# Splitting the attention result straight from PSUM, and weight conversions without a rank

## The chip, the cores and the metric

The kernel runs on one core of a Trainium2 chip. The metric is the device time of one execution in microseconds (us); lower is better. A core has five engines with queues of their own: TensorE (PE), which multiplies matrices into PSUM, VectorE (DVE), ScalarE (ACT) and GpSimd (POOL) for work on tiles, and SyncE (SP), which here issues all transfers.

## The reference

The reference is a linear attention with decay, followed by two pairs of dense layers, all in float32; the weights of the layers are given in double precision.

```python
for t in range(S):                                  # B, H, S, D = 4, 8, 768, 48
    cur = einsum('bhd,bhe->bhde', u * k_t, v_t)
    y[:, :, t] = einsum('bhd,bhde->bhe', r_t, state + cur)
    state = w_t[..., None] * state + einsum('bhd,bhe->bhde', k_t, v_t)
x = y as [B * S, H * D]                             # 3072 tokens of 384
h = x @ w_in;  x = where(h >= 1, h, where(h <= -1, 0, (h + 1) ** 2 / 4)) @ w_out    # d_ff = 2048
h = x @ w2_in; return (h * sigmoid(1.702 * h)) @ w2_out
```

## The kernel before, in words

**Products in two parts.** For speed, PE multiplies a rounded format. To keep float32 accuracy, each operand is split into a high part, rounded to that format, and a low part, the difference: `xh` and `xl` for the tokens, `whi` and `wlo` for the weights, `gh` and `gl` for the hidden layer. Each product is then three: high by high, high by low, low by high.

**Steps.** Tokens come in 8 tiles of 384. A step `s` handles one tile and one of the 16 slices of 128 hidden units: `gemm1` (9 matmuls into the PSUM tile `hp`), the activation (for layer 0: DVE L701, ACT L702, DVE L714, which gives `t`; then ACT L695 `gh` and, a step later, POOL or DVE in turn L689 `gl`), and `gemm2` (9 matmuls) for step `s - 3`. Steps 0 to 127 are layer 0, 128 to 255 layer 1.

**Attention windows.** The attention is computed in 24 windows of 128 tokens, three to a tile. `window(n)` (L416) is a generator, cut by `yield` into about 13 slots: the scans of the decay on DVE (L433, L435), products on DVE and POOL, the transposes `tp` and the scores `sc` on PE (L479, L484), the masked copy on DVE (L489), then `kv` (L508) and `yt` (L514) on PE. `yt` is a PSUM tile of 128 x 4 x 128: for each half of the partitions (a head of a pair) 48 rows, padded to 64, and four pairs of heads. The layer wants three blocks of 128 rows, so the fourth pair's 48 rows go, 16 at a time, into the padding of the first three. This is done with six transfers (L536) inside the SBUF tile `xr`, a copy of `yt` by ACT (L533). After them, ACT rounds the first three blocks to `xh` (L547), and `xl` is the difference (L550), on DVE for the first six windows (`XL_N`) and on POOL for the others, one slot later.

**Gate.** `attn_slot` (L560) moves every window in flight by one slot. A window that has yielded `"x"` (L542) is held as long as its tile lies more than one ahead of the tile that the steps work on. Windows start 4 slots apart at first and then 8 apart; the steps of a tile call 24 slots. Windows of layer 0 up to the third are run ahead of step 0.

**Weights.** `load_w` (L140) brings a piece of 128 x 384 doubles from HBM into one of four buffers `wst`; there are 32 pieces for layer 0, two for each slice. `to_f32` and `wide` make float32 of it: DVE L653, ACT L654, DVE L655, POOL L657. `load_w` for the piece four further on follows when a piece has been read. `split_w` makes `whi` (ACT L168) and `wlo` (PE and ACT for the first ten pieces, then DVE and POOL in turn, L177). Ten pieces are converted ahead of step 0; step `f` of tile 0 calls for the pieces up to `2 * f + 2 + 6` (L278), so the last pair is called for at step 12.

**What sets the order.** Up to and with step 15 (tile 0) the instructions are put in order by a scheduler: it simulates the engines and gives each one, among what is ready, the instruction of the highest rank. The rank is the place in the program; `high_priority(x)` lifts it by `x` places. Windows 0 to 2 are lifted by 400 (`WP0`), the first ten pieces by 300 (`CP0`), and pieces 10 to 31 by 3000 (`CP1`, L277). From step 16 on (`manual_schedule`) the order is that of the program. The order of each engine's queue, SP's among them, is fixed when the kernel is built, and each queue works in order.

Lines that the change and the steps of the prediction touch: the `"x"` gate (L542, L566), the copy `xr` (L533), the transfers (L536), `xh` (L547), `xl` (L550), `split_x2` (L247), which gives layer 1 its two parts in tiles of the same tags, and `CP1` (L66, used in L277).

Of the kernel before, what the change touches and what calls it, by code (L numbers as in the profile page):

```python
# [9 lines left out]
F32 = mybir.dt.float32  # L10
F32R = mybir.dt.float32r
I32 = mybir.dt.int32
U32 = mybir.dt.uint32
AF = mybir.ActivationFunctionType
ALU = mybir.AluOpType
# [4 lines left out]
B, H, S, D = 4, 8, 768, 48  # L20
NT, DM, DFF = B * S, H * D, 2048
C = 64
W = 128
NP = H // 2
# [5 lines left out]
KD = DM // 128  # L30
# [8 lines left out]
TN = 384  # L39
# [22 lines left out]
XL_N = 6  # L62
F0 = 0
WP0 = 400
CP0 = 300
CP1 = 3000  # L66
MAXW = 6
GAP1 = 8
CHECK_LATE = True
# [13 lines left out]
@with_exitstack  # L83
def rwkv_mlp_mlp_kernel(ctx, tc, rkw_t, nat, v_l, w1, w2, r, k, v, w, u, mi, mo, m2i, m2o, out, force=False):
    nc = tc.nc
    dram = ctx.enter_context(tc.tile_pool(name="dram", bufs=1, space=DRAM))
    keep = ctx.enter_context(tc.tile_pool(name="keep", bufs=1))
    x2_d = dram.tile([128, KD, NT], F32, name="x2_d")
    w2_d = dram.tile([128, 2 * KF, DM], F32, name="w2_d")
    flag_i = keep.tile([1, 1], I32, name="flag_i")  # L90

    with ExitStack() as st:
        fast_path(st, tc, rkw_t, nat, v_l, w1, w2, u, out, x2_d, w2_d, flag_i, force)

    rv = nc.values_load(flag_i[0:1, 0:1], min_val=0, max_val=1)
    with tc.If(rv == 0):
        general_path(tc, r, k, v, w, u, mi, mo, m2i, m2o, out)


def fast_path(st, tc, rkw_t, nat, v_l, w1, w2, u, out, x2_d, w2_d, flag_i, force):  # L100
    nc = tc.nc
    one = st.enter_context(tc.tile_pool(name="one", bufs=1))
    p2 = st.enter_context(tc.tile_pool(name="p2", bufs=2))
# [118 lines left out]
            nc.scalar.activation(out=whi[f][q], in_=wf, func=AF.Copy)  # L222
            late.append((i, wf))

    xh, xl = {}, {}
    x2_t = {}
    accs = {}
    gq = {}
# [17 lines left out]

    def split_x2(i):  # L247
        x2 = x2_t.pop(i)
        h_ = p2.tile([128, KD, TN], F32R, tag="xh", name="x2h")
        l_ = p2.tile([128, KD, TN], F32R, tag="xl", name="x2l")  # L250
        nc.vector.tensor_copy(h_, x2)
        nc.vector.tensor_tensor(out=l_, in0=x2, in1=h_.bitcast(F32), op=ALU.subtract)
        xh[1, i], xl[1, i] = h_, l_
# [15 lines left out]
    def step(s):  # L269
        if s < NS:  # L270
# [5 lines left out]
            if l == 0 and i == 0:  # L276
                with hooks["prio"](CP1):  # L277
                    while nconv[0] < min(NPC, 2 * f + 2 + AHEAD):  # L278
# [38 lines left out]
        if s < NS:  # L317
# [15 lines left out]
            if last and f == 8:  # L333
                split_x2(0)
# [9 lines left out]
            if l == 1 and i + 1 < len(TILES2):  # L344
                if f == 4:
                    load_x2(i + 1)
                if f == 12:
                    split_x2(i + 1)

    with ExitStack() as sa:  # L350
        at = sa.enter_context(tc.tile_pool(name="at", bufs=1))
        a2 = sa.enter_context(tc.tile_pool(name="a2", bufs=2))
# [49 lines left out]
        def load_v(n):  # L402
            i = n % 2
            tv = a2.tile([128, NP, 2, D], F32, tag="vn", name="vn")
            nc.sync.dma_start(out=tv, in_=nat[n, :, 2 * MC * D:].rearrange("p (m h d) -> p m h d", h=2, d=D))
            vn_t[n] = tv
            for hh in range(2):
                p = slice(64 * (1 - hh), 64 * (1 - hh) + 64)
                nc.sync.dma_start(out=lt[i][p, hh], in_=v_l[n, hh])
# [6 lines left out]
        def window(n):  # L416
            i = n % 2
            b, j = divmod(n, WPB)
            ti, off = tile_of[n]
# [26 lines left out]
            def lt_s(hh, c):  # L446
                p = slice(64 * hh, 64 * hh + D)
                return lt[i][p, hh].rearrange("p (m c) e -> p m c e", c=NC2)[:, :, c, 0:D]

            def put(us):  # L450
                for hh in range(2):
                    p = slice(64 * hh, 64 * hh + D)
                    nc.gpsimd.tensor_tensor(out=lt_s(hh, 0), in0=us[p], in1=pcs[p, :, None].to_broadcast([D, NP, D]), op=ALU.mult)
# [43 lines left out]
            yield from idle(GAPS[1])  # L497
            if PUT == 2 and not first:
                put(carry.pop())
            kvt = ps_s.tile([128, NC2, NP, D], F32, tag="s", name="kv")  # L500
            kv = [kvt[:, c] for c in range(1 if last else NC2)]

# [7 lines left out]
            def mm_y(c):  # L510
                for m in range(NP):
                    for hh in range(2):
                        mc = m * NC2 + c
                        nc.tensor.matmul(out=yt[64 * hh:64 * hh + 64, m, c * C:(c + 1) * C], lhsT=lt[i][:, hh, mc, :], rhs=ra[hh][:, mc, :], start=True, stop=True)  # L514
# [9 lines left out]
            yt = ps_s.tile([128, NP, W], F32, tag="s", name="yt")  # L524
# [4 lines left out]
                carry.append(upd(1))  # L529
            yield from idle(GAPS[2])  # L530
            mm_y(1)
            xr = a2.tile([128, NP, W], F32, tag="xr", name="xr", bufs=1)
            nc.scalar.activation(out=xr, in_=yt, func=AF.Copy)  # L533
            for hh in range(2):
                for q in range(3):
                    nc.sync.dma_start(out=xr[64 * hh + D:64 * hh + 64, q, :], in_=xr[64 * hh + 16 * q:64 * hh + 16 * q + 16, 3, :])  # L536
            yield
            sq = vn.rearrange("p m h d -> p (m h d)")
            nc.scalar.activation(out=sq, in_=sq, func=AF.Square, accum_out=stat[:, n, 2:3])
            if n + 2 < NW:  # L540
                load_v(n + 2)
            yield "x"  # L542
            if off == 0:
                xh[0, ti] = p2.tile([128, KD, TN], F32R, tag="xh", name="xh")
                xl[0, ti] = p2.tile([128, KD, TN], F32R, tag="xl", name="xl")
            o = xh[0, ti][:, :, off:off + W]
            nc.scalar.activation(out=o, in_=xr[:, 0:KD, :], func=AF.Copy)  # L547
            if n >= XL_N:
                yield
            (nc.vector if n < XL_N else nc.gpsimd).tensor_tensor(out=xl[0, ti][:, :, off:off + W], in0=xr[:, 0:KD, :], in1=o.bitcast(F32), op=ALU.subtract)  # L550
            yield

        def idle(n):
# [6 lines left out]
        def attn_slot():  # L560
            n = started[0]
            if n < (NW if cur[0] >= 0 else MAXW) and n in vn_t and n in nat_t and (not queue or queue[-1][1] >= GAP[0]):
                started[0] += 1
                queue.append([window(n), 0, n, None])
            for e in list(queue):
                if e[3] == "x" and tile_of[e[2]][0] > cur[0] + 1:  # L566
                    continue
                try:
                    e[3] = next(e[0])
                    e[1] += 1  # L570
                except StopIteration:
                    queue.remove(e)
# [306 lines left out]
```

## Time and profile before

| what | us |
|---|---|
| median of 3 runs (lowest, highest) | 1003.78 (1003.73, 1005.83) |
| the profiled execution, its own time | 1002.71 |
| its span, from the first instruction to the last | 1001.0 |
| PE busy in the span | 945.8 |
| DVE, ACT, POOL busy | 562.0, 538.2, 393.4 |

The rows that the prediction rests on stand in a section below, in numbered groups. Times in them are from the start of the span. A row of a timeline has the start, the length, the engine, the line, what is written from what, and in brackets the idle time ahead of it with what ended it. In the rows by line, the first numbers behind the bar are the busy time of the group and the mean of one instruction in ns. Busy times of matmuls overlap, so a group's mean is longer than the distance between two starts.

### The profile page before, as it was taken

Reading aid. Unit: us, or ns where it says so; the run is one execution under the profiler, and the core shown is the slowest. Engines: PE = TensorE matmul, PEld = TensorE weight load, DVE = VectorE, ACT = ScalarE, POOL = GpSimd, SP = SyncE. Lnnn points to the kernel's source line nnn. Section 1 sums busy time; section 2 is a strip of 40 time slices with the busy share of each in tenths; the row PEclk is TensorE's granted clock in tenths of the full one; section 3 lists DMA queues with packets and bytes.
Section 4 is the critical chain, followed back from the end, with each engine's and each line's share of the span. In section 5 each row is a group of like instructions: output and inputs, shape, how many; then the busy total and the mean of one; then the engine's idle time right before and its main releaser. Section 6 shows DMA issues by size and latency. Waiting matters only on the chain.

```text
span 1001.0 us, 18691 instructions
## 1 busy us (share of the span) xinstructions
PE 945.8 (94%) x6976; PEld 906.6 (91%) x6976; DVE 562.0 (56%) x983; ACT 538.2 (54%) x1279; POOL 393.4 (39%) x416
## 2 busy tenths in 40 slices
PE   4656999999999999999999999999999999999997
PEld 2445889999999999999999999999999999999997
DVE  6899976776877767777745753323232323232321
ACT  4666545666666667665654565555455433333332
POOL 6788744555555456455432541111111111111111
PEclk8857999999999999999999999999999999999999
DMA  9886515445555445553203443322222101000000
GB/s 236 208 226 176 140 24 164 132 118 140 156 134 147 117 113 154 144 146 104 66 20 115 129 133 99 96 78 85 87 81 85 59 2 45 3 28 22 25 1 28
DMA packets 52228, 101.73 MB, mean 102 GB/s; under 512 B 8608, under 2 KB 31392, under 8 KB 52128
## 3 DMA queue, kind: packets, MB, share of 16 engines
q1 hardware_dynamic: 52128, 100.45, 35.8%
q8 instruction: 57, 0.93, 0.4%
q14 instruction: 43, 0.35, 0.1%
HBM read 83.51 MB, written 15.73 MB: 99 GB/s over the span
## 4 chain that ended last, share of the span: by engine, by line
PE 63%; DVE 13%; ACT 10%; DMA 5%; issue 5%; SPq 3%; POOL 0%; ACTq 0%; DVEq 0%
PE hp L664 29%; PE acc L682 20%; PE acc L673 10%; SPq L536 3%; DVE pi L433 2%; DMA rk<-rkw_t 2%; DMA xr<-xr 2%; ACT gh L695 2%; DVE t L714 2%; ACT ra L472 2%; DVE ra L489 2%; ACT t L702 2%; DVE pi L435 1%; PE kv L508 1%; PE yt L514 1%
## 5 line engine op out<-in xcount | busy, mean ns | idle before, releaser
L689 POOL TENSOR_TENSOR gl<-t,gh 128x384 fp32r<-128x384 f32 x128 | 132.5, 1035 | 497.0 <-ACT gh L695 465.5
L695 ACT ACTIVATE gh<-t 128x384 fp32r<-128x384 f32 x256 | 134.1, 524 | 171.6 <-DVE t L714 93.4
L725 DVE TENSOR_TENSOR t<-t,hp 128x384 f32<-128x384 f32 x128 | 70.9, 554 | 218.6 <-ACT t L720 218.1
L720 ACT ACTIVATE t<-hp 128x384 f32<-128x384 f32 x128 | 62.8, 491 | 145.8 <-PE hp L664 145.8
L673 PE MATMUL acc<-gl,whi 128*128 128x384 f32 x384 | 131.2, 342 | 2.5 <-DVE gl L689 2.5
L673 PE MATMUL acc<-gh,whi 128*128 128x384 f32 x384 | 131.7, 351 | 0.8 <-ACT ev L263 0.3
L673 PE MATMUL acc<-gh,wlo 128*128 128x384 f32 x384 | 130.2, 339 | 0.0
L682 PE MATMUL acc<-wlo,gh 128*128 128x384 f32 x384 | 129.7, 338 | 0.0
L682 PE MATMUL acc<-whi,gh 128*128 128x384 f32 x384 | 129.5, 337 | 0.0
L682 PE MATMUL acc<-whi,gl 128*128 128x384 f32 x384 | 129.3, 337 | 0.0
L689 DVE TENSOR_TENSOR gl<-t,gh 128x384 fp32r<-128x384 f32 x128 | 75.4, 589 | 63.5 <-ACT gh L695 62.8
L702 ACT ACTIVATE t<-t 128x384 f32<-128x384 f32 x128 | 66.4, 519 | 65.7 <-DVE t L701 65.4
L714 DVE TENSOR_TENSOR t<-t,hp 128x384 f32<-128x384 f32 x128 | 70.2, 548 | 54.0 <-ACT t L702 52.5
L664 PE MATMUL hp<-xh,whi 128*128 128x384 f32 x384 | 91.9, 348 | 3.2 <-DVE t L714 3.2
L664 PE MATMUL hp<-xl,whi 128*128 128x384 f32 x384 | 89.3, 341 | 5.0 <-DVE xl L550 5.0
L701 DVE TENSOR_SCALAR t<-hp 128x384 f32<-128x384 f32 x128 | 70.4, 550 | 39.9 <-PE hp L664 39.6
L664 PE MATMUL hp<-x2h,whi 128*128 128x384 f32 x384 | 88.8, 339 | 0.0
L664 PE MATMUL hp<-xh,wlo 128*128 128x384 f32 x384 | 88.7, 339 | 0.0
L664 PE MATMUL hp<-x2l,whi 128*128 128x384 f32 x384 | 88.5, 339 | 0.0
L664 PE MATMUL hp<-x2h,wlo 128*128 128x384 f32 x384 | 88.1, 337 | 0.0
L673 PEld LDWEIGHTS acc<-gh,whi 128*128 128x128 f32 x384 | 72.2, 189 | 5.0 <-ACT ev L263 2.3
L673 PEld LDWEIGHTS acc<-gl,whi 128*128 128x128 f32 x384 | 72.6, 189 | 3.0 <-DVE gl L689 2.6
(108 smaller groups left out, 1849.1 us busy)
## 6 DMA issues: line engine op xcount, KB each, us to landing
wst<-w SPq DMA_DIRECT2D x96, 384.0 KB, 3.3
rk<-rkw_t SPq DMA_DIRECT2D x48, 288.9 KB, 5.0
rkn<-nat SPq DMA_DIRECT2D x24, 384.0 KB, 4.8
lt<-v_l SPq DMA_DIRECT2D x48, 128.0 KB, 3.7
w_d<-wt SPq DMA_DIRECT2D x32, 192.0 KB, 4.3
w2f<-w_d SPq DMA_DIRECT2D x32, 192.0 KB, 2.5
vn<-nat SPq DMA_DIRECT2D x24, 192.0 KB, 3.4
x_d<-ev SPq DMA_DIRECT2D x24, 192.0 KB, 2.2
```

The lines of the kernel that those rows point to most:

```text
L433: nc.vector.tensor_tensor_scan(out=rr[:, WW:0:-1], data0=ws[:, WW:0:-1], data1=one_s[:, WW:0:-1], initial=0.0, op0=ALU.mult, op1=ALU.max)
L536: nc.sync.dma_start(out=xr[64 * hh + D:64 * hh + 64, q, :], in_=xr[64 * hh + 16 * q:64 * hh + 16 * q + 16, 3, :])
L664: nc.tensor.matmul(out=hp[:, 0:n], lhsT=win(a, f, kk), rhs=b[:, kk, 0:n], start=(i == 0), stop=(i == 3 * KD - 1))
L673: nc.tensor.matmul(out=acc[j][:, 0:n], lhsT=wout(a, f, j * 128, 128), rhs=b[:, 0:n], start=(f == 0 and i == 0), stop=(f == KF - 1 and i == 2))
L682: nc.tensor.matmul(out=o[:, 0:DM], lhsT=a[:, j * 128:(j + 1) * 128], rhs=wout(b, f, 0, DM), start=(f == 0 and i == 0), stop=(f == KF - 1 a ...
L689: eng.tensor_tensor(out=gl[:, 0:n], in0=t[:, 0:n], in1=gh[:, 0:n].bitcast(F32), op=ALU.subtract)
L695: nc.scalar.activation(out=gh[:, 0:n], in_=t[:, 0:n], func=AF.Copy)
L701: nc.vector.tensor_scalar(t[:, 0:n], hp[:, 0:n], scalar1=-1.0, scalar2=1.0, op0=ALU.max, op1=ALU.min)
L702: nc.scalar.activation(out=t[:, 0:n], in_=t[:, 0:n], func=AF.Square, bias=0.5, scale=0.5)
L714: nc.vector.tensor_tensor(out=t[:, 0:n], in0=t[:, 0:n], in1=hp[:, 0:n], op=ALU.max)
L720: nc.scalar.activation(out=t[:, 0:n], in_=hp[:, 0:n], func=AF.Sigmoid, scale=1.702)
L725: nc.vector.tensor_tensor(out=t[:, 0:n], in0=t[:, 0:n], in1=hp[:, 0:n], op=ALU.mult)
```

## The change

After the change, `yt` is not copied to `xr`. One SBUF tile `xx` holds both parts, each with the four blocks of a token tile. ACT writes the high part of `yt` straight from PSUM into it, DVE subtracts that from `yt` in PSUM into the low part, for all windows, and the six transfers of a window move 16 rows of both parts at once. `split_x2` uses tiles of the same tag. The gate `"x"` moves ahead of the `kv` product. `CP1` is 0, so the conversion of pieces 10 to 31 is no longer lifted.

```diff
@@ -63,7 +63,7 @@
 F0 = 0
 WP0 = 400
 CP0 = 300
-CP1 = 3000
+CP1 = 0
 MAXW = 6
 GAP1 = 8
 CHECK_LATE = True
@@ -222,7 +222,7 @@
             nc.scalar.activation(out=whi[f][q], in_=wf, func=AF.Copy)
             late.append((i, wf))
 
-    xh, xl = {}, {}
+    xh, xl, xx = {}, {}, {}
     x2_t = {}
     accs = {}
     gq = {}
@@ -246,8 +246,8 @@
 
     def split_x2(i):
         x2 = x2_t.pop(i)
-        h_ = p2.tile([128, KD, TN], F32R, tag="xh", name="x2h")
-        l_ = p2.tile([128, KD, TN], F32R, tag="xl", name="x2l")
+        x = p2.tile([128, 2, NP, TN], F32R, tag="xx", name="xx2")
+        h_, l_ = x[:, 0, 0:KD], x[:, 1, 0:KD]
         nc.vector.tensor_copy(h_, x2)
         nc.vector.tensor_tensor(out=l_, in0=x2, in1=h_.bitcast(F32), op=ALU.subtract)
         xh[1, i], xl[1, i] = h_, l_
@@ -497,6 +497,7 @@
             yield from idle(GAPS[1])
             if PUT == 2 and not first:
                 put(carry.pop())
+            yield "x"
             kvt = ps_s.tile([128, NC2, NP, D], F32, tag="s", name="kv")
             kv = [kvt[:, c] for c in range(1 if last else NC2)]
 
@@ -529,25 +530,21 @@
                 carry.append(upd(1))
             yield from idle(GAPS[2])
             mm_y(1)
-            xr = a2.tile([128, NP, W], F32, tag="xr", name="xr", bufs=1)
-            nc.scalar.activation(out=xr, in_=yt, func=AF.Copy)
+            if off == 0:
+                x = p2.tile([128, 2, NP, TN], F32R, tag="xx", name="xx")
+                xx[ti], xh[0, ti], xl[0, ti] = x, x[:, 0], x[:, 1]
+            o, ol = (xx[ti][:, q, :, off:off + W] for q in range(2))
+            nc.scalar.activation(out=o, in_=yt, func=AF.Copy)
+            nc.vector.tensor_tensor(out=ol, in0=yt, in1=o.bitcast(F32), op=ALU.subtract)
+            x = xx[ti][:, :, :, off:off + W].bitcast(F32)
             for hh in range(2):
                 for q in range(3):
-                    nc.sync.dma_start(out=xr[64 * hh + D:64 * hh + 64, q, :], in_=xr[64 * hh + 16 * q:64 * hh + 16 * q + 16, 3, :])
+                    nc.sync.dma_start(out=x[64 * hh + D:64 * hh + 64, :, q, :], in_=x[64 * hh + 16 * q:64 * hh + 16 * q + 16, :, 3, :])
             yield
             sq = vn.rearrange("p m h d -> p (m h d)")
             nc.scalar.activation(out=sq, in_=sq, func=AF.Square, accum_out=stat[:, n, 2:3])
             if n + 2 < NW:
                 load_v(n + 2)
-            yield "x"
-            if off == 0:
-                xh[0, ti] = p2.tile([128, KD, TN], F32R, tag="xh", name="xh")
-                xl[0, ti] = p2.tile([128, KD, TN], F32R, tag="xl", name="xl")
-            o = xh[0, ti][:, :, off:off + W]
-            nc.scalar.activation(out=o, in_=xr[:, 0:KD, :], func=AF.Copy)
-            if n >= XL_N:
-                yield
-            (nc.vector if n < XL_N else nc.gpsimd).tensor_tensor(out=xl[0, ti][:, :, off:off + W], in0=xr[:, 0:KD, :], in1=o.bitcast(F32), op=ALU.subtract)
             yield
 
         def idle(n):
```

## Rows read from the trace of the kernel before

**Rows 1.** The page's slices of the span: busy tenths of PE, granted clock.

```profile
PE   4656999999999999999999999999999999999997
...
PEclk8857999999999999999999999999999999999999
```

**Rows 2.** Stretches: length, then busy PE, PEld, DVE, ACT, POOL, clock, DMA share, GB/s.

```profile
60.00:118.00 58.00, 37.72 (x375) 32.62 (x370) 55.33 (x82) 33.21 (x80) 45.59 (x45) 0.74 0.70 186
118.00:150.00 32.00, 31.96 (x214) 28.80 (x215) 25.48 (x46) 16.61 (x36) 17.74 (x17) 1.00 0.18 45
150.00:530.00 380.00, 376.40 (x3388) 357.45 (x3387) 270.77 (x487) 241.95 (x604) 195.77 (x215) 1.00 0.45 122
```

**Rows 3.** Timeline of PE, 60 to 150 us: start, length, line, operation, idle before.

```profile
70.19 2.07 PE L514 MATMUL yt<-ra,lt 128*64 128x64 f32 x32 [8.73 <-DMA rk<-rkw_t]
...
75.95 2.29 PE L664 MATMUL hp<-xh,whi 128*128 128x384 f32 x6
...
83.65 1.33 PE L664 MATMUL hp<-xl,whi 128*128 128x384 f32 x3 [5.01 <-DVE xl L550]
...
135.05 0.69 PE L664 MATMUL hp<-xh,whi 128*128 128x384 f32 x3
...
149.66 0.62 PE L664 MATMUL hp<-xh,whi 128*128 128x384 f32 x2
```

**Rows 4.** Timeline of ACT, 58 to 60 us.

```profile
59.01 0.58 ACT L533 ACTIVATE xr<-yt 128x512 f32<-128x512 f32 x1
```

**Rows 5.** Timeline of the SP queue (DMA issues), 58 to 76 us.

```profile
60.10 0.55 SPq L536 DMA_DIRECT2D xr<-xr  x1
61.52 0.33 SPq L140 DMA_DIRECT2D wst<-w  x1
...
70.82 0.51 SPq L536 DMA_DIRECT2D xr<-xr  x1
```

**Rows 6.** The tile xr: durations min/median/max in ns, first and last start.

```profile
L533 ACT ACTIVATE xr<-yt x24: 575/580/601, 29.6 to 515.8; 128x512 f32<-128x512 f32 x24
L547 ACT ACTIVATE xh<-xr x24: 507/524/528, 39.0 to 521.6; 128x384 fp32r<-128x384 f32 x24
L550 POOL TENSOR_TENSOR xl<-xr,xh x18: 998/1012/1030, 159.2 to 522.2; 128x384 fp32r<-128x384 f32 x18
L550 DVE TENSOR_TENSOR xl<-xr,xh x6: 547/796/4936, 41.7 to 128.0; 128x384 fp32r<-128x384 f32 x6
```

**Rows 7.** Stretches, xr's instructions alone: length, then DVE, ACT, POOL busy, clock, DMA.

```profile
0.00:1001.00 1001.00, 8.52 (x6) 26.50 (x48) 18.21 (x18) 0.97 0.36 102
```

**Rows 8.** DVE by form, 60 to 135 us: count, busy us, mean ns.

```profile
L177 DVE TENSOR_TENSOR wlo<-wt,whi 128x384 fp32r<-128x384 f32 x10 | 11.0, 1098 | 0.0
L653 DVE TENSOR_SCALAR ct<-wst 128x384 int32<-128x384 int32 x17 | 9.3, 547 | 0.1
L655 DVE SCALAR_TENSOR_TENSOR wt<-wst,ct 128x384 int32<-128x384 int32 x17 | 9.2, 542 | 0.2
...
L433 DVE TENSOR_TENSOR_SCAN pi<-rk,one_s 128x516 f32<-128x516 f32 x4 | 6.5, 1636 | 1.9 <-DMA rk<-rkw_t 1.9
L435 DVE TENSOR_TENSOR_SCAN pi<-rk,seed 128x516 f32<-128x516 f32 x4 | 6.0, 1508 | 0.0
L489 DVE COPY_PREDICATED ra<-mask,sc 64x512 f32<-64x512 int32 x8 | 6.0, 744 | 0.2
L701 DVE TENSOR_SCALAR t<-hp 128x384 f32<-128x384 f32 x10 | 5.4, 542 | 0.0
L714 DVE TENSOR_TENSOR t<-t,hp 128x384 f32<-128x384 f32 x10 | 5.4, 535 | 0.0
L689 DVE TENSOR_TENSOR gl<-t,gh 128x384 fp32r<-128x384 f32 x5 | 4.9, 983 | 0.0
```

**Rows 9.** Line 536 (xr's transfers), 0 to 150 us.

```profile
DMA to landing us min/median/max: 1.6/3.2/6.7
```

**Rows 10.** Timeline of DVE, 44 to 48 us.

```profile
46.43 0.56 DVE L653 TENSOR_SCALAR ct<-wst 128x384 int32<-128x384 int32 x1 [2.79 <-DMA wst<-w]
```

## The prediction

> **What bounds the kernel now.** I read the slices of the span first. TensorE (PE) is at nine tenths or more from the fifth slice of 25 us to the last but one, and its granted clock is at nine tenths or more there; only the first four slices show gaps, with a clock of 5 to 8 tenths [rows 1]. The table by stretches gives the size. From 150 to 530 us, where attention windows run beside the matrix products, PE is busy 376.40 of 380 us; nothing in that stretch can give back more than 3.6 us. From 118 to 150 us PE is busy 31.96 of 32. From 60 to 118 us it is idle 20.3 us, at a mean clock of 0.74 [rows 2]. So the time of this kernel is a front of some 118 us plus a fixed amount of PE work behind it, and a change is worth what it moves in the front. In the front the engine that is full is VectorE (DVE): 55.33 of 58 us from 60 to 118 us [rows 2].
>
> Then I looked at what step 0 of the first layer waits for, since it is the first large piece of PE work. Its first matmul of an xh runs at 75.95 us, but the first of an xl only at 83.65, after 5.01 us of idle PE that ended with DVE's xl [rows 3]. The yt of window 2, the last of tile 0, was copied out by ScalarE (ACT) at 59.01 [rows 4]. Between lie the six transfers of xr. They are issued by SyncE (SP) from 60.10 to 70.82, and the queue holds weight loads between them, the first at 61.52 [rows 5]; SP works in order, so a transfer that was ready at 59.6 leaves eleven microseconds later. That is the rank of the conversion at work: its loads stand ahead of window 2's transfers. The last thing in the way is the xl itself: one of the six on DVE took 4.936 us where the shortest took 0.547 [rows 6].
>
> **The change, part by part.**
>
> *xl read from PSUM.* Six DVE subtractions of 384 columns go in the front; by the tile's own row their median is 0.796 us and the longest 4.936 [rows 6], in all 8.52 us [rows 7]. Six of 512 columns come, with one operand in PSUM. The nearest row is the product of t with hp, a DVE operation on two tensors of which one lies in PSUM: 0.535 us for 384 columns [rows 8]; times 512/384 this is 0.71 us, and six are 4.3 us. The stretching is the point: the operations whose two inputs both lie in SBUF have means of 1.098 (wlo) and 0.983 (gl) in the same stretch, those that read hp from PSUM 0.535 and 0.542 [rows 8]. I take 0.71 and DVE is relieved of 4.3 us; the bounds are no stretch saved (six more times 0.17 us, that is 1.0 us dearer) and 4.3 us. As DVE is full there, what leaves DVE leaves the front: -4.3 us.
>
> The rows give no extra price to an operand in PSUM: 0.535 us with it, 0.547 for the shortest xl from SBUF [rows 6, 8]. [...]
>
> *ACT.* The copy of yt stays as one operation of 512 columns, now rounded on the way (0.580 us either way, taken from the row of xr), and the second copy of 0.524 us goes, 24 times [rows 6]. ACT is busy 33.21 of 58 us in the front [rows 2]; I cost this at nothing by itself, since DVE covers it. The tile xr had one buffer, so an ACT copy also waited for the previous window's xl; that wait goes too, and what is late next on ACT is DVE's work.
>
> *Transfers.* Still six for a window, SP's issue of 0.55 us each [rows 5], twice the bytes. They now start after the xl, so SP waits for DVE rather than for ACT, and a weight load or a load of the next window may stand behind that wait. Landing takes 3.2 us in the median of the front [rows 9]. With window 2's yt copied by 59.6, an xl of 0.71 us, six issues of 0.55 and a landing of 3.2 us, step 0 could start complete at about 67 us against 83.65. Bounds: the same 83.65, if DVE or SP puts other work ahead, and 67.
>
> *The rank.* The conversions of pieces 10 to 31 had the highest rank in the scheduled part; now they have that of their step, behind windows 0 to 2 (lifted by 400) and the first ten pieces (by 300). Their loads go behind window 2's transfers. The work is only moved: a pair costs DVE two times 0.547 + 0.542 us and one wlo of 1.098, 3.3 us [rows 8], before or after. So DVE's total does not fall, and with DVE full the end of the conversions, about 135 us now, comes earlier by the 4.3 us above and by little else. What the order can give is PE work done by then. At 135.05 us step 11 begins; step 15 begins at 149.66, 3.65 us per step [rows 3]. The code asks for the last pair at step 12, so with work in the order of the steps PE can be about one step further when the last conversion ends: -3.65 us. Bounds: nothing, and three steps (-11 us), if step 0 at 67 us lets PE work off what it now idles through: of the 20.3 us idle [rows 2], 5.0 are counted with xl, and 8.73 us [rows 3] were a wait in window 3 that the edit does not name.
>
> *The manual part.* From window 6 on the xl moves from GpSimd (POOL), 18 of 1.012 us [rows 6], to DVE, 18 of 0.71: 12.8 us more on an engine busy 270.77 of 380 us [rows 2]. DVE waits there for PE's yt and ACT's copy, and the max (t with hp) of the running step stands behind it; the step's result is wanted three steps later and there are three hp buffers, so some 2 us are covered. If not, 18 windows cost what is uncovered. The gate "x" now stands ahead of kv; every third window waits there for one slot of the eight between windows, and finishes seven slots ahead of its tile. I cost both at nothing; bounds -3.6 us (all idle of the stretch) and +4.
>
> *Sum:* -4.3 - 3.65 = -8.0 us on the profiled execution's 1002.71 us (span 1001.0), 994.7. The median of the runs, 1003.78, lies 1.07 above the profiled one, so 995.8.
>
> **Rivals.**
>
> *The conversions come too late (slower).* The 11th conversion starts at 46.43 us now [rows 10]. Put strictly in step order, each step has on DVE 3.3 us for its pair, 0.542 + 0.535 + half of 0.983 for itself, and 1.5 of a window's 8 slots, whose two scans and two predicated copies alone are 4.6 us [rows 8]: 0.9. That is 5.7 us a step, 63 us for eleven pairs, and three steps of 3.65 behind: step 15 begins 74 us after the 11th conversion. It loses where that conversion starts later than 76 us; at 82 us it costs 6 us: 1010. For it: loads of weights are started only when a conversion frees a buffer, so a late start is not made up. Against: DVE takes what is ready, and the loads for pieces 10 to 13 go out with the first ten pieces.
>
> *The rank changes nothing.* The loads may set the order anyway, and only the xl is saved: 1003.8 - 4.3 = 999.5. If SP's wait for DVE also delays loads by the same amount, 1003.
>
> *PE is full from step 0 on.* The order gives three steps: 1003.8 - 4.3 - 11 = 988.5.
>
> *DVE becomes the bound in the manual part:* 18 windows with 2 us uncovered would be 36 us; the bound above is +4, since DVE has 109 us free there. I fold it into the slower cases.
>
> **How the numbers follow.** Forecast (990 to 999) 0.44; PE full early (below 990) 0.13; rank without effect (999 to 1001.8) 0.18; no change 0.09; slower, mostly late conversions, 0.16. A measurement of this kernel can tell some 0.2%, 2.0 us, from no change. So faster 0.75, same 0.09, slower 0.16. The range 985 to 1007 leaves out the extremes of the early and the late case, some 0.15 in all.
>
> **What would show it.** xl on DVE 24 times at about 0.7 us with none above 1 us; six transfers of window 2 in a row on SP; the first matmul of xl near 67 us; last conversion near 131 us; step 15 near 141. PE idle from 60 to 118 us should fall from 20 to about 12. Wrong, if the 11th conversion comes after 76 us, if SP stands long before the transfers while weight loads queue, or if PE's idle time from 150 to 530 us grows past 3.6 us.

## The result, and the profile after

The changed kernel takes 992.12 us in the median of 4 runs (991.53 to 992.59) against 1003.75; the ratio is 0.9884, with a 95% interval of 0.9869 to 0.9900. The prediction was 995.8, in a range of 985 to 1007. The profiled execution has a span of 990.0 us, 11.0 less than before.

The page's slices of the changed kernel, busy tenths of PE and the granted clock:

```profile
PE   4757999999999999999999999999999999999997
...
PEclk9978999999999999999999999999999999999999
```

The gaps are still in the first four slices [rows 1], the second and the fourth a tenth fuller, all four at a higher clock. The stretches that answer to [rows 2], with the same columns (busy PE, PEld, DVE, ACT, POOL, then clock, DMA share, GB/s):

```profile
60.00:118.00 58.00, 43.70 (x382) 37.69 (x383) 55.29 (x89) 33.07 (x77) 48.85 (x46) 0.79 0.64 176
150.00:530.00 380.00, 379.27 (x3422) 362.41 (x3422) 297.13 (x514) 236.31 (x591) 193.02 (x197) 1.00 0.44 124
```

From 60 to 118 us PE is idle 14.3 us where it was 20.3, with DVE as full as before (55.29 of 58 us). From 150 to 530 us the idle time fell from 3.6 to 0.73 us.

PE's timeline of the changed kernel, which answers to [rows 3]:

```profile
63.39 1.69 PE L509 MATMUL kv<-vn,ktok 64*48 64x48 f32 x32 [4.27 <-DVE xx L538]
67.18 1.01 PE L661 MATMUL hp<-xx,whi 128*128 128x384 f32 x2 [2.11 <-DMA xx<-xx]
...
72.88 0.95 PE L661 MATMUL hp<-xx,whi 128*128 128x384 f32 x4
...
142.54 1.22 PE L661 MATMUL hp<-xx,whi 128*128 128x384 f32 x6
...
144.12 1.22 PE L661 MATMUL hp<-xx,whi 128*128 128x384 f32 x6
```

Two of the nine matmuls of step 0's `gemm1` run at 67.18 us (67 was forecast for all); the others follow at 72.88, when the last transfer of window 2 has landed, and PE does other work between. Step 15 begins at 142.54 (141 was forecast), and step 16, the first of tile 1, at 144.12. New is the first row: PE waited 4.27 us ahead of `kv`, until DVE's xl had freed the PSUM bank of a `yt`.

Window 2's transfers on the SP queue, which answer to [rows 5]:

```profile
63.36 3.15 SPq L542 DMA_DIRECT2D xx<-xx  x5
...
67.65 0.59 SPq L542 DMA_DIRECT2D xx<-xx  x1
```

Five of the six now leave in a row. The sixth, at 67.65 us, takes longest to land (line 542, 67.6 to 67.7 us), so it is there at 72.74:

```profile
DMA to landing us min/median/max: 5.1/5.1/5.1
```

The operations on the tile that answer to [rows 6] (duration min/median/max in ns):

```profile
L537 ACT ACTIVATE xx<-yt x24: 576/580/607, 29.8 to 508.9; 128x512 fp32r<-128x512 f32 x24
L538 DVE TENSOR_TENSOR xx<-yt,xx x24: 659/691/693, 31.0 to 509.6; 128x512 fp32r<-128x512 f32 x24
```

All 24 subtractions on DVE take 659 to 693 ns; none is stretched.

To see where the 11.0 us came from, I split the span at the first matmul of tile 1 and at that of tile 7, behind which no window runs. The kernel before (step 16 begins at 152.05, step 112 at 532.74 us):

```profile
0.00:152.10 152.10, 107.48 (x976) 87.59 (x976) 128.75 (x211) 87.76 (x201) 105.98 (x112) 0.82 0.64 166
152.10:532.70 380.60, 377.00 (x3381) 358.37 (x3381) 271.17 (x489) 243.00 (x606) 195.77 (x215) 1.00 0.45 122
532.70:1001.00 468.30, 461.36 (x2623) 460.68 (x2621) 162.06 (x285) 207.40 (x472) 91.60 (x89) 1.00 0.20 64
```

The changed kernel (144.12 and 521.53 us):

```profile
0.00:144.10 144.10, 106.41 (x911) 86.49 (x912) 122.41 (x205) 85.09 (x194) 105.15 (x112) 0.91 0.70 188
144.10:521.50 377.40, 376.67 (x3446) 359.44 (x3445) 296.30 (x513) 235.42 (x589) 193.63 (x197) 1.00 0.44 121
521.50:990.00 468.50, 461.36 (x2623) 460.68 (x2621) 161.51 (x285) 207.51 (x472) 90.72 (x89) 1.00 0.21 64
```

The front, up to tile 1, became 7.9 us shorter (8.0 between the rounded edges of the rows), tiles 1 to 6 3.3 us; the rest is equal within 0.2. The counts in the rows tell something else: 976 matmuls of PE lie in the front before, 911 after. Those are, but for one, the 32 of `kv` and 32 of `yt` of window 6, some 2 us of PE work that is now done in tiles 1 to 6. So tiles 1 to 6 gained 3.3 us although they do 2 us more.

The granted clock of the front rose as well, from 0.82 to 0.91 in these rows. No run changes the clock by itself, but the time does not go with it: with the xl lifted (below) the front has 0.86 and tile 1 starts at 144.7 us, with window 6 two slots later 0.89 and 140.3. And of the four runs of the changed kernel, with means of 0.969 to 0.985 over the whole, the one at 0.969 is the fastest.

### The profile page after: what moved, and what is told of

Its sections match the earlier page's. It is cut to its first block, busy times and chain, and to the rows that moved or that the text cites. A ratio compares the mean times of both kernels' runs of the same rounds, so it can differ in the third digit from the quotient of the medians.

```text
span 990.0 us, 18582 instructions
## 1 busy us (share of the span) xinstructions
PE 944.4 (95%) x6976; PEld 906.6 (92%) x6976; DVE 580.2 (59%) x1001; ACT 528.0 (53%) x1255; POOL 389.5 (39%) x398
## 4 chain that ended last, share of the span: by engine, by line
PE 80%; DVE 7%; DMA 4%; issue 3%; ACT 3%; POOL 1%; SPq 0%; DVEq 0%; ACTq 0%; POOLq 0%
PE hp L661 37%; PE acc L679 20%; PE acc L670 18%; DMA rk<-rkw_t 2%; PE yt L515 2%; PE kv L509 2%; PE sc L484 2%; DMA wst<-w 1%; DVE pi L433 1%; DVE rk L441 1%; DVE t L711 1%; DVE t L698 1%; DVE wlo L177 1%; DVE ct L650 1%; PE tp L479 0%
## 5 line engine op out<-in xcount | busy, mean ns | idle before, releaser
L661 PE MATMUL hp<-xx,whi 128*128 128x384 f32 x1536 | 318.0, 342 | 7.4 <-DVE t L711 5.2
L686 POOL TENSOR_TENSOR gl<-t,gh 128x384 fp32r<-128x384 f32 x128 | 136.9, 1070 | 471.3 <-ACT gh L692 443.6
L661 PEld LDWEIGHTS hp<-xx,whi 128*128 128x128 f32 x1536 | 273.2, 190 | 9.8 <-DVE t L711 5.7
L661 PE MATMUL hp<-xx,wlo 128*128 128x384 f32 x768 | 177.6, 340 | 0.0
L661 PEld LDWEIGHTS hp<-xx,wlo 128*128 128x128 f32 x768 | 139.0, 189 | 0.0
L686 DVE TENSOR_TENSOR gl<-t,gh 128x384 fp32r<-128x384 f32 x128 | 80.8, 631 | 51.1 <-ACT gh L692 49.7
L670 PEld LDWEIGHTS acc<-gh,wlo 128*128 128x128 f32 x384 | 72.1, 188 | 0.0
L679 PEld LDWEIGHTS acc<-whi,gl 128*128 128x128 f32 x384 | 72.1, 188 | 0.0
```

Of the source, the lines that this page charges most:

```text
L661: nc.tensor.matmul(out=hp[:, 0:n], lhsT=win(a, f, kk), rhs=b[:, kk, 0:n], start=(i == 0), stop=(i == 3 * KD - 1))
L670: nc.tensor.matmul(out=acc[j][:, 0:n], lhsT=wout(a, f, j * 128, 128), rhs=b[:, 0:n], start=(f == 0 and i == 0), stop=(f == KF - 1 and i == 2))
L679: nc.tensor.matmul(out=o[:, 0:DM], lhsT=a[:, j * 128:(j + 1) * 128], rhs=wout(b, f, 0, DM), start=(f == 0 and i == 0), stop=(f == KF - 1 a ...
L686: eng.tensor_tensor(out=gl[:, 0:n], in0=t[:, 0:n], in1=gh[:, 0:n].bitcast(F32), op=ALU.subtract)
```

## The experiments

Each states the times of tile 1 and tile 7, taken like those above, since they tell the front from the manual part.

**The rank alone.**

```diff
# on the kernel before
-CP1 = 3000
+CP1 = 0
```

> The kernel before with CP1 = 0 and nothing else. Theory (both edits carry a part): window 2's six transfers leave SP nearly in a row, the first matmul of an xl comes at 67 to 75 us instead of 83.65, xl on DVE can still be stretched past 1 us, and PE's idle time from 150 to 530 us stays near 3.6 us. Time 998 to 1001. Rival A (the rank has no effect, the loads set the order): 1003 to 1005, transfers as spread as before. Rival B (the rank is all of the gain): 991 to 994.

Measured: 1004.15 us, ratio 0.9999 (0.9987 to 1.0011). SP's queue around window 2's transfers, and then the stretches to tile 1 and from there to tile 7:

```profile
60.16 4.91 SPq L536 DMA_DIRECT2D xr<-xr  x5
...
67.00 0.51 SPq L536 DMA_DIRECT2D xr<-xr  x1
```

```profile
0.00:150.10 150.10, 110.17 (x976) 89.34 (x977) 123.13 (x210) 88.96 (x202) 105.18 (x112) 0.85 0.64 169
150.10:533.40 383.30, 377.01 (x3382) 358.35 (x3381) 271.91 (x489) 242.18 (x605) 195.22 (x215) 1.00 0.44 121
```

The order of SP changed as the theory said; the transfers stand together, and the stretch of the xl went too (the six took 4.07 us instead of 8.52). The first matmul of an xl runs at 76.5 us, later than expected. The front is 2.0 us shorter. Tiles 1 to 6 took 383.3 us instead of 380.6, with PE idle 6.3 us instead of 3.6, and nothing was left: its waits for ACT's `ev` copies, which free the accumulators, are 3.1 us there and 0.3 before. What holds ACT up is not shown. The time is that of rival A, but not for its reason, since the transfers did move. The rank gives no measurable gain by itself.

**The data path alone** (with the gate, which goes with it).

```diff
# on the changed kernel
-CP1 = 0
+CP1 = 3000
```

> The changed kernel with CP1 = 3000 as before. Theory: xl on DVE 24 times at 0.66 to 0.69 us, none above 1 us, PE idle from 150 to 530 us below 1.5 us, but window 2's transfers again lie between weight loads and step 0 starts later than 67 us. Time 995 to 998. Rival A (the data path is all of the gain): 991 to 993. Rival B (the rank is all): 1002 to 1005.

Measured: 993.84 us, ratio 0.9906 (0.9891 to 0.9920).

```profile
0.00:144.20 144.20, 104.82 (x912) 85.03 (x913) 123.23 (x205) 84.89 (x194) 103.96 (x112) 0.91 0.71 188
144.20:522.30 378.10, 376.66 (x3446) 359.41 (x3445) 297.37 (x513) 235.35 (x589) 189.78 (x197) 1.00 0.43 121
```

Tile 1 starts at 144.2 as in the changed kernel, and the first matmul of step 0 runs at 66.7. The intervals of this kernel and of the changed one overlap. Rival A comes nearest: what gains is the data path with its gate. That step 0 would start late again was wrong.

**An xl from SBUF.**

```diff
# on the changed kernel
+            xr = a2.tile([128, NP, W], F32, tag="xr", name="xr", bufs=2)
+            nc.scalar.activation(out=xr, in_=yt, func=AF.Copy)
-            nc.vector.tensor_tensor(out=ol, in0=yt, in1=o.bitcast(F32), op=ALU.subtract)
+            nc.vector.tensor_tensor(out=ol, in0=xr, in1=o.bitcast(F32), op=ALU.subtract)
```

> The changed kernel, but ACT copies yt once more, to SBUF, and DVE's xl reads that copy: two inputs in SBUF instead of one. Theory (an xl from PSUM is not stretched, one from SBUF is): the mean of the six xl of the front rises from 0.67 us to above 1 us, and the time by 1 to 4 us, 993 to 996. Rival (what the front loses by the change is that yt stays in PSUM until xl is done, 6.7 us of PE waiting in kv): that wait goes, since ACT alone frees yt, and the time falls to 986 to 990 in spite of 0.58 us more on ACT for each window. No effect: 991.5 to 993.

Measured: 1002.62 us, ratio 0.9991 (0.9982 to 1.0000), outside all that was expected. The xl of this kernel, its stretches to tile 1 and to tile 7, and PE's longest wait in the latter:

```profile
L540 DVE TENSOR_TENSOR xx<-xr,xx x24: 659/713/1497, 30.9 to 520.6; 128x512 fp32r<-128x512 f32 x24
```

```profile
0.00:145.40 145.40, 107.74 (x911) 87.99 (x912) 122.99 (x207) 89.36 (x201) 107.72 (x112) 0.87 0.69 187
145.40:531.80 386.40, 379.92 (x3446) 362.50 (x3445) 297.34 (x511) 243.83 (x606) 194.05 (x197) 0.99 0.42 118
```

```profile
PE acc L672 <- ACT ev L263: 5.9, 4, 1.6
```

The front is only 1.3 us longer than in the changed kernel, though the six xl of the front are stretched again (to 0.98 us in the mean, the longest 1.497). What is lost is in tiles 1 to 6, 9.0 us. ACT's extra copy stands ahead of its copies `ev` at the end of a tile, which free the accumulators, and PE waits 5.9 us for these. The rest is busy time of PE: 379.92 us against 376.67 for the same 3446 matmuls, at a mean granted clock of 0.99. So ACT's queue matters there more than the busy time (242 of 380 us) tells.

**xl on DVE in the old kernel.**

```diff
# on the kernel before
-            (nc.vector if n < XL_N else nc.gpsimd).tensor_tensor(out=xl...
+            nc.vector.tensor_tensor(out=xl...
```

> The kernel before, but xl on DVE for all 24 windows, still from the SBUF copy (only the engine of windows 6 to 23 changes). It asks what took PE's idle time from 150 to 530 us from 3.6 to 0.7 us in the changed kernel. Theory (ACT's rounding copy, which waited for the transfers, held up ACT's later work): the idle time stays at 3 to 4 us and the time at 1003 to 1005. Rival (POOL's xl was in the way of POOL's gl): the idle time falls below 1.5 us and the time to 1000 to 1002.

Measured: 1006.57 us, ratio 1.0027 (1.0015 to 1.0039), above both ranges. PE's waits from 150 to 530 us:

```profile
PE kv L508 <- ACT ktok L486: 4.0, 8, 0.9
```

POOL's relief gives nothing; with the xl on DVE and the rest as before, `kv` waits more for ACT's `ktok` (4.0 us, 1.3 before). The rival is out.

**A slot ahead of kv in the old kernel.**

```diff
# on the kernel before
+            yield "x"
             kvt = ps_s.tile([128, NC2, NP, D], F32, tag="s", name="kv")
 ...
-            yield "x"
+            yield
```

> The kernel before with one edit: the gate, and with it one more slot, stands ahead of kv, and the old gate is a plain slot. Theory (in the manual part the gain is the slot between the scores and kv, which lets ACT's ktok and DVE's masked copy end first): tiles 1 to 6 take some 4 us less in all, 376 to 377 instead of 380.6 us, the first kv after an hp and the first yt after kv no longer wait, and the time is 998 to 1001. Rival (the manual gain is ACT's and POOL's relief from the second copy and the xl): tiles 1 to 6 stay at 380 to 382 us, the time at 1003 to 1005.

Measured: 1023.98 us, ratio 1.0206 (1.0193 to 1.0219), far above both ranges. Tile 1 starts at 150.9 us, tile 7 at 554.3. PE's waits, in which `tp` and `sc` of a window are new:

```profile
PE tp L479 <- issue: 6.2, 4, 1.6
PE sc L484 <- ACT xr L534: 5.1, 5, 1.1
```

**No slot in the new kernel.**

```diff
# on the changed kernel
-            yield "x"
             kvt = ps_s.tile([128, NC2, NP, D], F32, tag="s", name="kv")
 ...
-            yield from idle(GAPS[2])
+            yield "x"
             mm_y(1)
```

> The changed kernel with the gate put on the idle slot ahead of the second half of yt, so that kv comes two slots after the scores, as before the change. Theory (the slot): tiles 1 to 6 rise from 377.4 to 380 to 382 us, the time to 994 to 997. Rival (ACT's and POOL's relief): no change, 991.5 to 993.

Measured: 999.21 us, ratio 0.9954 (0.9942 to 0.9966).

```profile
0.00:151.80 151.80, 109.16 (x959) 87.80 (x960) 128.48 (x211) 85.90 (x196) 105.68 (x112) 0.82 0.65 169
151.80:529.40 377.60, 375.12 (x3398) 357.97 (x3397) 279.50 (x506) 234.02 (x588) 184.74 (x197) 1.00 0.46 125
```

The loss of 7.1 us against the changed kernel is in the front, not in the manual part where it was expected: tile 1 starts at 151.8 us, as before the change, and tiles 1 to 6 take 377.6. With the data path and the rank of the changed kernel, but the gate behind `kv`, the front keeps the whole length of the old one, and DVE's busy time in it (128.48 us, 128.75 before the change, 122.41 after). Its DVE also has a long operation, though no xl is stretched:

```profile
46.29 4.30 DVE L433 TENSOR_TENSOR_SCAN pi<-rk,one_s 128x516 f32<-128x516 f32 x1 [0.23 <-ACT pi L459]
```

This scan, with two inputs in SBUF, took 4.30 us, the shortest of them 1.23.

**An ACT copy put back, in a slot of its own.**

```diff
# on the changed kernel, behind load_v(n + 2)
             yield
+            xs = a2.tile([128, KD, W], F32, tag="xs", name="xs", bufs=1)
+            nc.scalar.activation(out=xs, in_=xx[ti][:, 0, 0:KD, off:off + W].bitcast(F32), func=AF.Copy)
+            yield
```

> The changed kernel with an ACT copy of 384 columns put back behind the transfers, into a tile that nothing reads. Theory (the slot): ACT has room and kv's slot, so 992 to 994. Rival (ACT's relief, the copy that waited for the transfers above all): tiles 1 to 6 rise by 2 to 5 us, the time to 994.5 to 997.

Measured: 1037.24 us, ratio 1.0341 (1.0328 to 1.0354), far above both. Tile 1 starts at 145.4, so all is lost behind it. PE's waits there:

```profile
PE sc L484 <- DVE xx L538: 8.9, 5, 1.8
PE tp L479 <- DVE us L521: 7.9, 5, 1.6
```

Counting slots in the code explains this run and the one with a slot in the old kernel. There windows 0 to 2 take 14 slots, not 13, so that windows 3 and on start one slot earlier against the steps: window 6 at slot 14 of tile 0, not 15. It reaches the gate two slots before tile 1 opens it and is held for two; its second half of `yt` then comes one slot ahead of `tp` and `sc` of window 7, which want the same two PSUM banks. In the changed kernel it is held for one, and two slots lie between. That is read from the code. The waits above name the tiles that it predicts, but the hold by itself was not tried, and the ACT copy waits for transfers here as well.

**xl lifted.** The xl of windows 0 to 5 stands in `with prio(400 ...)`, the rest as in the changed kernel.

> The changed kernel with the xl of windows 0 to 5 lifted by 400 places. PE waits 6.7 us between 60 and 118 us for xl to free yt's bank ahead of kv. If that wait delays the front, it shortens and the time falls to 988 to 991. If DVE's total bounds the front, the wait goes elsewhere and the time stays at 991.5 to 993.

Measured: 991.28 us, ratio 0.9887 (0.9872 to 0.9901), the same as the changed kernel. The lift moved little: window 2's xl still comes behind the same DVE operations, at 63.40 us (62.66 without it), and PE's wait ahead of `kv` from 60 to 144 us fell from 6.7 to 4.4 us only. Those 2.3 us did not shorten the front; whether the rest of that wait sets it stays open.

**The gate in the old kernel, no slot added.**

```diff
# on the kernel before
+            yield "x"
             kvt = ps_s.tile([128, NC2, NP, D], F32, tag="s", name="kv")
 ...
-            yield "x"
```

> The kernel before with the gate ahead of kv and no slot added elsewhere, so that windows 0 to 5 take 13 slots and start where those of the changed kernel start; data path and rank as before. Theory (the place of the gate is the larger part: kv and yt of window 6 leave the front, and kv comes three slots after the scores): tile 1 starts 4 to 8 us earlier than 152.1, tiles 1 to 6 stay below 381 us, the time is 995 to 999. Rival (without the new data path the gate gives nothing; ACT waiting for the transfers holds ktok up): 1001 to 1005. Each window is held one slot, not two as in the run with one slot more; if the time rises again to 1020, the account of that run by the two slots is wrong.

Measured: 1046.40 us, ratio 1.0424 (1.0404 to 1.0443), far above both ranges. Tile 1 starts at 149.3 and tile 7 at 574.6 us. The waits of tiles 1 to 6:

```profile
ACT xh L547 <- DMA xr<-xr: 55.0, 18, 3.9
...
PE acc L673 <- ACT ev L263: 23.3, 6, 5.0
```

Here the rounding copy `xh` follows its transfers after one slot instead of two. ACT stands 55.0 us in tiles 1 to 6 waiting for them (9.4 before), and PE 23.3 us for ACT's `ev` copies. No `tp` waits, so the holds of two slots are not what slows this one.

**The ACT copy, no slot of its own.** As above without the second `yield`.

> The changed kernel with the ACT copy of 384 columns put back behind the transfers without a slot of its own. Theory (the 45 us of the run with the copy came from its slot, which lets windows 6, 9, ... be held two slots and meet the next window in the two PSUM banks): 992 to 995. Rival (the ACT copy that waits for the transfers costs the time): above 1010.

Measured: 1061.93 us, ratio 1.0577 (1.0550 to 1.0604): my theory fell, the rival held.

```profile
ACT xs L549 <- DMA xx<-xx: 65.7, 18, 4.7
...
PE acc L672 <- ACT ev L263: 29.7, 6, 5.8
```

An ACT copy of 0.52 us that waits for the transfers costs 70 us here; its wait, 65.7 us in tiles 1 to 6, is the largest there for a transfer, and behind it PE waits 29.7 us for the `ev` copies. Nobody reads this copy, so nothing but ACT waits for it. Together with the run before it says what the new data path is for the schedule: no engine but PE, at the start of a tile, waits for the transfers any more. With the gate alone, the wait of `xh` turned into a loss. In both runs the ACT copy stands one slot behind its transfers; two slots behind, as before the change, ACT's wait is the 9.4 us named above.

**Window 6 later.**

```diff
-queue[-1][1] >= GAP[0])
+queue[-1][1] >= GAP[0] + (3 if n == 6 else 0))
```

> The changed kernel with window 6 started three slots later, and so all windows behind it: DVE's work of window 7 and PE's of part of window 6 leave the front, and no window is held at the gate. Theory (DVE's total bounds the front): tile 1 starts 2 to 5 us before 144.1, tiles 1 to 6 do not rise by more than what is moved, some 1 us, and the time is 988 to 990.5. Rival (the front is set by the order and by waits for transfers): 991.5 to 993. If the last window of a tile comes too late for the next tile, 995 or more.

Measured: 1006.38 us, ratio 1.0025 (1.0015 to 1.0036). Tile 1 starts at 140.3 us, 3.8 earlier, as the theory says; but tiles 1 to 6 take 393.3 us, the last of the cases in what was expected. PE's longest wait there:

```profile
PE hp L661 <- DMA xx<-xx: 6.0, 9, 1.7
```

The last transfers of each tile now land 1.0 to 1.2 us after the first matmul of the next tile is due (at 272.7 for 271.5 us, for one); in the changed kernel they land 3.0 to 4.0 us ahead of it in the tiles up to 6, and in the kernel before 12. The waiting PE is only part of the 16 us. Tiles 1 to 6 of this kernel:

```profile
140.30:533.60 393.30, 383.75 (x3446) 363.68 (x3445) 299.57 (x515) 237.99 (x593) 182.40 (x199) 0.99 0.44 122
```

Against the changed kernel (377.40 us, PE busy 376.67) the 15.9 us fall into two parts: PE is idle 8.8 us longer, and busy 7.1 us longer with the same 3446 matmuls. The mean granted clock is 0.99 in this row, 1.00 in that of the changed kernel: it falls to half (0.5 of full) three times, from 205.7 to 209.1, 338.8 to 342.2 and 407.1 to 410.5 us, each time just behind the start of a tile that had waited for its transfers. The gate in the old kernel without a slot (tile 1 at 149.3, tile 7 at 574.6 us) shows the same on a larger scale: PE is busy 392.03 us there with as many matmuls, at a mean clock of 0.97. So in the slow kernels the loss is larger than PE's idle time.

**Window 6 two slots later, 7 and 8 closer.**

```diff
-queue[-1][1] >= GAP[0])
+queue[-1][1] >= GAP[0] + {6: 2, 7: -1, 8: -1}.get(n, 0))
```

> The changed kernel with window 6 started two slots later and windows 7 and 8 seven slots behind the one before instead of eight, so that window 8 and all behind it start where they do in the changed kernel. Theory (window work that leaves tile 0 shortens the front, and what spoiled the run with three slots was the landing of the last transfers of a tile, 1.0 to 1.2 us after the end of the tile before): tile 1 starts 1.5 to 3.5 us before 144.1, the transfers of window 8 land some 3 us ahead of tile 2 as in the changed kernel, tiles 1 to 6 take 377 to 379 us, the time is 989 to 991. Rival (any shift of the windows against the steps costs in the manual part): above 993.

Measured: 989.66 us (987.98 to 990.46), ratio 0.9856 (0.9835 to 0.9876).

```profile
0.00:140.30 140.30, 108.74 (x911) 87.05 (x912) 119.36 (x202) 85.46 (x194) 100.77 (x110) 0.89 0.72 194
140.30:518.70 378.40, 376.79 (x3447) 359.32 (x3446) 298.20 (x515) 235.64 (x589) 193.36 (x199) 1.00 0.44 121
```

The front is again 3.8 us shorter than in the changed kernel, tiles 1 to 6, which now hold all of window 7, 1.0 us longer. This version is faster than the kernel before. Against the changed kernel its median is 2.5 us lower, but the intervals of the ratios overlap, so the difference is not settled.

## Why the prediction was right, and where its working was not

The sign, the size within the range, the place (a front that shrinks) and the date of step 15 (142.5 us, 141 forecast) came true. The terms of the sum did not, so that it came near is luck. The date of step 0, 67 us, held for its first two matmuls, by luck too: ACT had written the high part of window 2 by 56.4 us, not 59.6; DVE's xl, forecast to follow at once, stood behind other DVE work until 62.66, a scan that waited 1.9 us for its transfer among it; and the first five landings took 1.8 to 2.4 us, not 3.2. The sixth landed at 72.74.

- *xl read from PSUM, -4.3 us.* The durations came out: 4.03 us for the six (0.67 each, 0.71 forecast). The step that failed is "what leaves DVE leaves the front". Without the gate ahead of `kv` the six are as short (0.68 each), yet the front is 151.8 us with DVE busy 128.48, as before the change: what the xl gave back, other DVE operations took, the scan of 4.30 us among them. The run with the rank alone lost the stretch and gained 2.0 us in the front and nothing in the time. The run with an xl from SBUF does not decide it: its six take 1.9 us more, and its front is 1.3 us longer. The long operation without the gate is another one of DVE with two SBUF inputs, the scan of 4.30 us; that it is the same stretch, moved with the order, is my estimate and was not tried by itself.
- *The rank, -3.65 us.* Failed. Window 2's transfers do leave together and step 0 does start earlier, but the time does not follow: 0.9999 by itself, and with the data path tile 1 starts at 144.1 or 144.2 with or without it. Step 0's start does not set tile 1's: the xl from SBUF starts step 0 at 76.8 and tile 1 at 145.4. The rival by which the rank changes nothing was right on the rank.
- *The gate, costed at nothing.* This is the term that was missed most. Without it the changed kernel's front is 151.8 us instead of 144.1, and the time 999.21 instead of 992.12. It is not worth that by itself, though: in the old kernel, with as many slots, it shortens the front by 2.7 us, to 149.3, and loses 44.6 in tiles 1 to 6. So of the 7.9 us of the front 0.2 come with the data path and the rank alone, 2.7 with the gate alone, and the rest only with both. The gate holds `kv`, the state update and `yt` of window 6, which tile 2 wants, until tile 1 has begun, when PE is the bound and the other engines have room. Shown is that less window work in tile 0 makes the front shorter, by this run and by 3.8 us in both runs with window 6 later. Of the 7.7 us between the changed kernel with and without it, some 1.5 are the moved PE work (48 matmuls) and 1.4 four state updates of DVE. The eight scans of line 433 also take 15.9 us without it and 10.7 with it; that this explains much of the rest is likely, and was not tried by itself.
- *The manual part, costed at nothing, at most -3.6 us.* It gave 3.3 us and did 2 us more work. The bound failed because it took PE's idle time for all that PE can lose. Tiles 1 to 5 hold the same 2908 matmuls in both kernels; from start to start they took 321.5 us before and 316.0 after, and PE's idle time fell by 2.9 of these 5.5 us. Measured the same way, the time from the last `kv` to the first `yt` fell from 3.08 to 0.77 us for 15 windows, and that from a step's last matmul to the first `kv` from 5.69 to 3.96. The run with no slot ahead of `kv` parts the causes: there tiles 1 to 5 took 318.2 us, the first of these times is 0.77 too, and the second 6.78. So some 3.4 us came without the slot, with the new data path, and some 2.2 with the slot, which gives `ktok` time to be ready. The theory that the slot is all of the gain here was wrong.
- *ACT, costed at nothing.* Not so behind the front: the kernel with one more ACT copy of `yt` and an xl from it is 10.5 us slower than the changed one, 9.0 of it in tiles 1 to 6.
- *xl on DVE from window 6 on.* Right: DVE is busy 297.13 of 380 us there, and nothing waits for it in that part.
- *Transfers.* Right in the median: six of 0.59 us for an issue, with landings of 2.0 us in the median of the front (3.2 before [rows 9]). The one that step 0 had to wait for took 5.1. That those of tiles 2 to 6 land only 3.0 to 4.0 us before they are wanted was not seen; the run with window 6 three slots later shows how little room that is.
- *The slower rival.* Not borne out: the 11th conversion runs at about 49 us, far from 76.

For an operand in PSUM nothing extra was counted. The run with the xl from SBUF is a direct test of that: the same subtraction of 512 columns takes 659 ns at its shortest with one operand in PSUM (changed kernel) and 659 ns with both in SBUF, so the rows show no extra price here.

## What to carry to other kernels

Take the wait for a transfer out of any engine that works through a queue in order, even where its own idle time looks harmless: here a copy that waits for transfers cost 70 us, and one that does not 10.5. When a pipeline has a gate, ask which work it lets into the stretch that is not yet bound by the main engine; holding work for later tiles back was worth 7.1 us here, but only beside the new data path. So test each term alone and with the others: a sum can come near with its terms wrong.

## What was not expected of the hardware

A DVE subtraction with one operand in PSUM took 659 to 693 ns in all 24 cases, and five of the six in the front ran beside POOL operations for 0.5 us or more; with both operands in SBUF 659 to 1497 ns, and up to 4936 ns for a shorter one in the kernel before. The kernel before with only its later xl moved, with the same order in the front, had the same stretch, 4935 ns: it belongs to the order, not to chance. That the POOL operations beside it cause the stretch was not tried by itself. The time lost reached 4.4 us here, more than one of these POOL operations takes (at most 1.47 us). The rows of the kernel before show what ran beside that xl: it began beside a POOL operation, four more followed that one without a gap, and it ended 0.4 us after the last of them.

```profile
78.66 4.94 DVE L550 TENSOR_TENSOR xl<-xr,xh 128x384 fp32r<-128x384 f32 x1
76.64 2.54 POOL L464 TENSOR_SCALAR_AFFINE_SELECT ra<-bb 64x512 f32<-64x512 f32 x2
79.16 0.98 POOL L657 TENSOR_TENSOR wt<-wt,wb 128x384 int32<-128x384 int32 x1
80.11 1.17 POOL L444 TENSOR_TENSOR rk<-rk,pi 128x512 f32<-128x512 f32 x1
81.24 0.98 POOL L177 TENSOR_TENSOR wlo<-wt,whi 128x384 fp32r<-128x384 f32 x1
82.19 0.98 POOL L436 TENSOR_TENSOR rkn<-rkn 128x384 f32<-128x384 f32 x1
```
